# Seven block products for the second expert layer: transposed products, sums per batch, weight blocks kept in DRAM

## The chip, the cores and the metric

The kernel runs on one core of a Trainium2 chip. The metric is device time in microseconds (us), the median of several executions; lower is better. Beside it there is one profiled execution, from which all durations come.

## The reference

Two stages follow one another. The first is attention over 4 batches, 8 heads, 768 positions and head size 64, where a key is kept if it is one of the first `n_global` (8) or among the last `n_local` (96) positions, with a linear distance bias per head. The second is a mixture of four experts on every token: `x` is the attention output as a matrix of 3072 tokens by 512.

```python
p = domain_probs / (domain_probs.sum(-1, keepdims=True) + 1e-09)
for e in range(E):                       # E = 4
    h = np.maximum(x @ w1[e], 0.0)       # 512 -> 1024
    out += p[:, e:e + 1] * (h @ w2[e])   # 1024 -> 512
```

All is in float32. The two products with `w1` and `w2` are most of the arithmetic.

## The kernel before

**Split arithmetic.** A float32 factor is split into a high part (rounded to the matmul format fp32r by a copy on ScalarE) and a low part (the difference, by VectorE or GpSimd). A product is three matmuls: high by high, high by low, low by high. So every weight block and every block of `x` or `h` costs a copy and a subtraction before TensorE may use it.

**Units.** The expert stage goes batch by batch (768 tokens). A unit is one batch, one expert and one group of 256 of the 1024 hidden features; there are 16 units in a batch and 64 in all. `first(i)` makes the 256 hidden features of unit i for 768 tokens, `second(i)` multiplies them with the unit's 256 rows of `w2`.

**First product.** It goes by seven products of blocks (Strassen's scheme in Winograd's form): the 512x256 piece of `w1` is cut in four blocks, `load_w1` builds A11, A12, A22 and the sums S1 to S4 on GpSimd and splits them; `blocks(b)` builds and splits B11, B21, B22 and T1 to T4 of `x`. Each block product is six matmuls with 384 columns (`product`), so a unit has 42. VectorE adds the products up in `add`, four results go through ReLU on ScalarE (`relu`, which also makes the high part of `h`), and VectorE makes the low part (`work_late`).

**Second product.** It is plain: for each of six tiles of 128 tokens, six matmuls with 512 columns have `h` as the stationary side and `w2` as the moving one, so a unit has 36. VectorE multiplies the tile by the expert's share of the token and adds it to `acc`; six such accumulators belong to a batch, and they are written out after its last unit. `load_w2` fetches and splits the unit's `w2` anew for each batch, as `load_w1` does with `w1`.

**Order.** Attention of batch 0 runs first, in program order (`Ordered.on`). From then on the attention of batch b+1 is dealt out in small steps between the products of batch b, and the tile framework's planner, with its own costs, settles the order on each engine. Weight loads, transposed loads and all attention inputs are issued from SP's queue, the outputs from ScalarE's. In every batch the last products of the old batch stand before `blocks(b + 1)`, which has eight VectorE operations in front of the first products of the new one.

**Buffers.** PSUM has eight banks: three for the products (`pm`), two for scores (`ps`), two for transposes (`pt`), one for the attention output (`px`). The weights `w1s` and `w2s` have two buffers each.

Of the kernel before, what the change touches and what calls it, by code (L numbers as in the profile page):

```python
# [18 lines left out]
P = 128  # L19
# [166 lines left out]
def attn_moe_kernel(ctx: ExitStack, tc, q, k, v, n_global, n_local, domain_probs, w1, w2, out):  # L186
# [85 lines left out]
    wp = main.enter_context(tc.tile_pool(name="wp", bufs=2))  # L272
    rp = main.enter_context(tc.tile_pool(name="rp", bufs=1))

    class Pools:


        def __init__(self, stack, name, st, kd, qd, nat, natv, pb, ps, pt):
# [8 lines left out]
            self.pb, self.pT, self.small = sbuf("pb", pb), sbuf("pT", 4), sbuf("small", pb)  # L287
            self.ps, self.pt, self.px = psum("ps", ps), psum("pt", pt), psum("px", 1)

    def mixture():  # L290

        sy.dma_start(prob, domain_probs.rearrange("(t p) e -> p t e", p=P))
        yield
        psumm = fast.tile([P, NT, 1], F32, name="psumm")
        ve.reduce_sum(psumm, prob, axis=AX.X)
        ve.tensor_scalar_add(psumm, psumm, 1e-9)
        ve.reciprocal(psumm, psumm)
        for e in range(E):
            ve.tensor_mul(prob[:, :, e : e + 1], prob[:, :, e : e + 1], psumm)
# [16 lines left out]

    def transpose_half(A, nat, hf):
        tp = A.pt.tile([P, 512], F32, name="pt")
        for t in range(TPH):
            te.transpose(tp[:, t * P : (t + 1) * P], nat[:, hf * TPH + t].rearrange("p j d -> p (j d)"), ident)  # L320
        return tp

    def prepare_q(A, nat, hf, got):

        tp = transpose_half(A, nat, hf)
        st = A.st.tile([P, 2, HALF], F32R, name="st_q")
        ac.activation(st[:, 0, :], tp[:, :HALF], AF.Copy, scale=-SCALE)
        yield
# [8 lines left out]
    def prepare_k(A, nat, hf, got):  # L337


        tp = transpose_half(A, nat, hf)  # L340
# [8 lines left out]
        yield  # L349
# [6 lines left out]
    def prepare_early(A, nat, hf, name, got, zq):  # L356


        tp = transpose_half(A, nat, hf)
# [86 lines left out]
    def weigh(A, three, x):  # L446

        px = A.px.tile([P, 512], F32, name="px")
# [17 lines left out]
    def attention(b, A, early=False):  # L466
# [5 lines left out]
        def flow(new=None):  # L472

            one, two, three, four = tiles
            if new:
                new["ps"] = scores(A, new["t"], gots[new["pr"]], early)
            if three and not early:
                turn(A, three)
# [3 lines left out]
            if four:  # L482
                turned.append(four)
                if len(turned) == TPH:
                    weigh(A, turned, x)
                    turned.clear()
            tiles[:] = [new, one, two, three]

        def start(pr):

            nats[pr] = {n: next(load(A, src, b, pr, n)) for n, src in (("q", q), ("k", k), ("v", v))}

        def prepare(nat, got):

            got["v"] = nat
            q0, q1 = (prepare_q(A, nat["q"], hf, got) for hf in range(2))
            k0, k1 = (prepare_k(A, nat["k"], hf, got) for hf in range(2))
            next(q0)
            yield 1
            next(q0, None)  # L500
            next(k0)
            yield 1
            next(k0, None)
            yield 1
            next(k1)
            yield 1
            nat["vg"] = windows(A, nat["v"])
            next(k1, None)
            next(q1)
            yield 1  # L510
            next(q1, None)
# [72 lines left out]

    xb = {}

    def blocks(b, ks=(0, 1), low=ve):
# [7 lines left out]
        def high(name, src):  # L595
            if lo == 0:
                xb[name] = bp.tile([P, 2, 2, HALF], F32R, name=f"x{name}")
            ac.copy(xb[name][:, 0, lo:hi], src)

        def rest(eng, name, src):  # L600
            eng.tensor_tensor(xb[name][:, 1, lo:hi], src, f32(xb[name][:, 0, lo:hi]), op=ALU.subtract)

        high("B11", b11)
        high("B22", b22)
        ve.tensor_sub(b12, b22, b12)
        rest(po, "B22", b22)
        yield 1
        rest(low, "B11", b11)
        ve.tensor_add(b11, b12, b11)
        high("T2", b11)  # L610
        yield 1
        rest(low, "T2", b11)
        ve.tensor_sub(b22, b22, b11)
        high("T1", b22)
        yield 1
        rest(low, "T1", b22)
        high("T3", b12)
        yield 1
        rest(po, "T3", b12)
        high("B21", b21)  # L620
        ve.tensor_sub(b11, b21, b11)
        yield 1
        rest(po, "B21", b21)
        high("T4", b11)
        yield 1
        rest(low, "T4", b11)
# [3 lines left out]
    NPR = FF // (2 * P)  # L630
    units = [(b, e, g) for b in range(B) for e in range(E) for g in range(NPR)]
    wts = {}

    def load_w1(i, wait=0, lead=5, hold=2):


        if i >= len(units):
            return
        _, e, g = units[i]
        for _ in range(wait):  # L640
            yield 1
        raw = rp.tile([P, KT, 2 * P], F32, name="raw1")
        sy.dma_start(raw, w1[e, :, g * 2 * P : (g + 1) * 2 * P].rearrange("(a p) f -> p a f", p=P))
        for _ in range(lead):
            yield 1
        a11, a21 = raw[:, 0:2, :P], raw[:, 0:2, P:]
        a12, a22 = raw[:, 2:4, :P], raw[:, 2:4, P:]
        sums = rp.tile([P, 4, 2, P], F32, name="sums")
        s1, s2, s3, s4 = (sums[:, n] for n in range(4))
        po.tensor_add(s1, a21, a22)  # L650
        po.tensor_sub(s2, s1, a11)
        po.tensor_sub(s3, a11, a21)
        po.tensor_sub(s4, a12, s2)
        for _ in range(hold):
            yield 1
        dst = wp.tile([P, 2, 7, 2, P], F32R, name="w1s")
        wts[(i, 1)] = {name: dst[:, :, n] for n, name in enumerate(("A11", "A12", "A22", "S1", "S2", "S3", "S4"))}
        for sl, src in (
            (slice(0, 2), raw[:, :, :P].rearrange("p (n a) f -> p n a f", n=2)),
            (slice(2, 3), a22.rearrange("p (n a) f -> p n a f", n=1)),  # L660
            (slice(3, 5), sums[:, 0:2]),
            (slice(5, 7), sums[:, 2:4]),
        ):
            ac.copy(dst[:, 0, sl], src)
            po.tensor_tensor(dst[:, 1, sl], src, f32(dst[:, 0, sl]), op=ALU.subtract)
            yield 1

    def load_w2(i, lead=7):

        if i >= len(units):  # L670
            return
        _, e, g = units[i]
        raw = rp.tile([P, 2, DM], F32, name="raw2")
        sy.dma_start(raw, w2[e, g * 2 * P : (g + 1) * 2 * P, :].rearrange("(a p) m -> p a m", p=P))
        for _ in range(lead):
            yield 1
        dst = wp.tile([P, 2, 2, DM], F32R, name="w2s")
        wts[(i, 2)] = dst
        for f in range(2):
            ac.copy(dst[:, 0, f], raw[:, f])  # L680
            po.tensor_tensor(dst[:, 1, f], raw[:, f], f32(dst[:, 0, f]), op=ALU.subtract)
            yield 1

    hs = {}

    def product(i, a, x):

        pm = ps_mm.tile([P, 512], F32, name="pm")
        m = 0
        for kt in range(2):  # L690
            for wi, xi in ((0, 0), (1, 0), (0, 1)):
                te.matmul(
                    pm[:, :HALF], wts[(i, 1)][a][:, wi, kt, :], xb[x][:, xi, kt, :], start=(m == 0), stop=(m == 5)
                )
                m += 1
        return pm

    late = []

    def work_late():  # L700

        while late:
            lo, src, hi = late.pop()
# [174 lines left out]
```

## Time and profile before

| What | Value |
|---|---|
| median of 3 runs | 1233.19 us (1232.62 to 1234.7) |
| the profiled execution's own time | 1233.96 us |
| its span, first to last instruction | 1232.2 us |
| TensorE (PE) busy | 1182.1 us, 96% |
| VectorE (DVE) busy | 993.0 us, 81% |
| GpSimd (POOL) busy | 737.4 us, 60% |
| ScalarE (ACT) busy | 568.3 us, 46% |
| DMA moved | 117.22 MB, 95 GB/s |

In the rows below, PE is TensorE's matmul, PEld its weight load, DVE VectorE, ACT ScalarE, POOL GpSimd and SP the queue engine. A group's row names the tile written and those read (`pm<-w2s,h`), partitions by elements, the count, the busy time in us, the mean ns of one, and the idle time of the engine before it with what ended it. `xT` and `xB` are the blocks of `x`; `p`, `u`, `vv` and `c` the partial sums of the first product. Almost every row has line 42, that of the helper through which each operation is issued, so groups are told apart by tiles.

### The profile page before, as it was taken

How to read it: one execution, taken by the hardware profiler on the slowest of the kernel's cores; microseconds unless marked ns; L12 is line 12 of the kernel's file. 1: busy time of each engine (PE TensorE's matmuls, PEld its weight loads, DVE VectorE, ACT ScalarE, POOL GpSimd, SP SyncE). 2: the span in 40 equal slices, each digit the busy share in tenths (PEclk: the TensorE clock that was granted, in tenths of full speed). 3: DMA queues.
4: the chain of work that ended last, by engine and by line, in shares of the span. 5: the costliest groups of instructions: out<-in, count | busy, mean ns of one | idle time of the engine just before them, and what ended most of it. 6: DMA issues, size and time to landing. Idle time of an engine off the chain costs nothing.

```text
span 1232.2 us, 18808 instructions
## 1 busy us (share of the span) xinstructions
PE 1182.1 (96%) x6624; PEld 1052.2 (85%) x6624; DVE 993.0 (81%) x2018; ACT 568.3 (46%) x1332; POOL 737.4 (60%) x706
## 2 busy tenths in 40 slices
PE   6779999999999999999998999999999899999997
PEld 4558889889888899899897899889898799999996
DVE  6888898888978888887888887978787876666665
ACT  4764455554543554544543454554454333333321
POOL 5467655655575755655568655655656686666630
PEclk9989999999999999999999999999999999999999
DMA  6324343424324325242412433343331222222211
GB/s 160 103 56 117 94 121 95 121 84 124 94 74 145 103 79 141 78 139 81 126 56 78 149 108 99 105 114 106 100 90 57 103 69 69 69 69 69 69 35 54
DMA packets 142678, 117.22 MB, mean 95 GB/s; under 512 B 82672, under 2 KB 115440, under 8 KB 142576
## 3 DMA queue, kind: packets, MB, share of 16 engines
q1 hardware_dynamic: 138832, 109.65, 31.5%
q10 hardware_dynamic: 3744, 6.30, 1.3%
q8 instruction: 54, 0.88, 0.3%
q14 instruction: 48, 0.39, 0.1%
HBM read 86.03 MB, written 6.29 MB: 75 GB/s over the span
## 4 chain that ended last, share of the span: by engine, by line
PE 85%; DVE 12%; ACT 1%; issue 1%; DMA 0%; ACTq 0%; DVEq 0%
PE pm L42 75%; PE pt L42 4%; PE px L42 3%; DVE pb L42 3%; PE ps L42 3%; DVE h L42 2%; DVE acc L42 1%; DVE u L42 1%; DVE zsum L42 1%; DVE xT L42 1%; ACT pb L42 1%; DVE x L42 1%; DVE vv L42 1%; DVE c L42 0%; DVE early_q L42 0%
## 5 line engine op out<-in xcount | busy, mean ns | idle before, releaser
L42 PE MATMUL pm<-w2s,h 128*128 128x512 f32 x2304 | 557.3, 395 | 15.9 <-DVE acc L42 15.5
L42 PEld LDWEIGHTS pm<-w2s,h 128*128 128x128 f32 x2304 | 427.6, 189 | 109.9 <-DVE acc L42 21.9
L42 POOL TENSOR_TENSOR w1s<-raw,w1s 128x512 fp32r<-128x512 f32 (+1 forms) x128 | 156.1, 1238 | 272.8 <-ACT w1s L42 272.4
L42 DVE SCALAR_TENSOR_TENSOR acc<-pm,prob,acc 128x512 f32<-128x512 f32 x360 | 262.1, 744 | 64.2 <-PE pm L42 62.2
L42 PE MATMUL pm<-xT,w1s 128*128 128x384 f32 x1536 | 297.2, 338 | 3.4 <-DVE xT L42 1.8
L42 PEld LDWEIGHTS pm<-xT,w1s 128*128 128x128 f32 x1536 | 266.6, 188 | 8.1 <-DVE xT L42 2.7
L42 PE MATMUL pm<-xB,w1s 128*128 128x384 f32 x1152 | 228.3, 340 | 0.7 <-DVE xB L42 0.4
L42 PEld LDWEIGHTS pm<-xB,w1s 128*128 128x128 f32 x1152 | 201.7, 188 | 6.9 <-DVE xB L42 0.7
L42 POOL TENSOR_TENSOR w2s<-raw,w2s 128x512 fp32r<-128x512 f32 x128 | 164.9, 1308 | 65.6 <-ACT w2s L42 63.1
L42 POOL TENSOR_TENSOR w1s<-sums,w1s 128x512 fp32r<-128x512 f32 x128 | 167.9, 1331 | 3.3 <-ACT w1s L42 2.9
L42 ACT CAST w2s<-raw 128x512 fp32r<-128x512 f32 x128 | 73.8, 618 | 192.8 <-PE pm L42 183.3
L42 ACT ACTIVATE pb<-pb,nmax 128x256 f32<-128x256 f32 (+1 forms) x192 | 93.1, 486 | 109.1 <-DVE nmax L42 101.8
L42 POOL TENSOR_TENSOR sums<-raw 128x256 f32<-128x256 f32 x128 | 95.0, 763 | 65.1 <-DMA raw<-in_moe_w_dram 65.1
L42 DVE TENSOR_SCALAR pb<-pb,zsum 128x256 f32<-128x256 f32 (+1 forms) x192 | 111.3, 611 | 2.9
L42 ACT ACTIVATE h<-c 128x384 fp32r<-128x384 f32 x64 | 33.6, 525 | 113.0 <-DVE c L42 112.4
L42 DVE TENSOR_TENSOR u<-pm,p 128x384 f32<-128x384 f32 x64 | 35.6, 556 | 58.0 <-PE pm L42 52.4
L42 DVE CUSTOM_DVE_ANT_0 pb<-ps,nbias 128x256 f32<-128x256 f32 (+1 forms) x192 | 71.4, 394 | 7.2 <-PE pt L42 3.7
L42 ACT COPY pT<-pt 128x512 f32<-128x512 f32 (+1 forms) x96 | 52.2, 544 | 52.7 <-PE pt L42 52.4
L42 DVE SCALAR_TENSOR_TENSOR h<-u,h 128x384 fp32r<-128x384 f32 x64 | 66.9, 1046 | 10.0 <-ACT h L42 9.6
L42 ACT CAST w1s<-sums 128x512 fp32r<-128x512 f32 x128 | 74.0, 614 | 1.1 <-POOL sums L42 1.0
L42 DVE TENSOR_TENSOR u<-pm,u 128x384 f32<-128x384 f32 x128 | 70.4, 550 | 3.5 <-PE pm L42 2.9
L42 PE MATMUL pt<-ident,pb 128*128 128x128 f32 x352 | 57.6, 280 | 13.9 <-DVE pb L42 13.2
(87 smaller groups left out, 1276.8 us busy)
## 6 DMA issues: line engine op xcount, KB each, us to landing
raw<-in_moe_w_dram SPq DMA_DIRECT2D x128, 512.0 KB, 3.5
qd<-st_q SPq DMA_DIRECT2D x96, 192.0 KB, 3.5
v<-in_v_dram SPq DMA_DIRECT2D x16, 384.0 KB, 4.1
out_dram<-acc ACTq DMA_DIRECT2D x24, 256.0 KB, 2.3
q<-in_q_dram SPq DMA_DIRECT2D x30, 192.0 KB, 3.1
k<-in_k_dram SPq DMA_DIRECT2D x30, 192.0 KB, 3.6
vg<-v SPq DMA_DIRECT2D x16, 288.0 KB, 3.7
q<-in_q_dram SPq DMA_DIRECT2D x4, 96.0 KB, 3.2
```

The source lines that it names most:

```text
L42: ins = fn(*args, **kwargs)
```

## The change

- **Second product.** Two units make a chunk, 32 in all, eight a batch. `second(c)` multiplies transposed: a block of `w2` is stationary, `h` (features by 384 tokens) is moving. In batches 1 to 3 it goes by seven block products per chunk, of 12 matmuls with 384 columns each (`SCHEME`, `multiply`); in batch 0 it is plain, with 96 such matmuls per chunk.
- **Sums per batch.** Each of the seven products has its own sum in SBUF (`slot`), to which `collect` adds every chunk's product; the scheme's final additions (`FINAL`) are made once per batch. `output` then turns the result with 12 transposes per half batch on TensorE, copies it on ScalarE, and stores 768 KB at a time.
- **Hidden features.** `first` lets products add up in PSUM where it can, and one VectorE operation (`weighed`) does ReLU and the multiplication with the expert's share, which `load_mix` brings from DRAM, spread over all partitions. `hidden(k)` makes the block sums of `h` and splits each 768 wide block: a copy on ACT, and the difference on DVE (all of batch 0; T4 and T1 later) or on POOL (the other five).
- **Weight blocks.** The split blocks of `w1` are made in batch 0 only and those of `w2` in batch 1 only (`make_pair`); each pair of blocks is written to DRAM by a DMA from POOL (`keep`) and read back by SP's queue in the later batches (`pair_w1`, `next_w2`). A pair of `w1` has three buffers to turn in, one of `w2` four (two units by two pairs).
- **Block sums of x.** `blocks(b + 1)` gives one block per step, spread over the last seven steps of the batch before; the first six steps of the new batch's second products are put ahead of its first product (`ALONE`).
- **Attention.** The q and k inputs come in halves with three buffers; scores have one PSUM bank, `px` shares the two of the transposes, and the products have two banks (`ps_mm`) and three more (`y0`, `y1`, `z`).

```diff
-    def blocks(b, ks=(0, 1), low=ve):
+    def blocks(b, A, ks=(0, 1), low=po):
...
+        def split(name, src, eng):
+            high, rest = block(name)
+            ac.copy(high, src)
+            eng.tensor_tensor(rest, src, f32(high), op=ALU.subtract)
...
+    PAIRS1 = (("A11", "A12"), ("S2", "S1"), ("S3", "S4"), ("A22",))
+    PAIRS2 = (("A11", "A12"), ("S3", "A22"), ("S2", "S1"), ("S4",))
+    def split_pair(dst, src):
+        ac.copy(dst[:, 0], src)
+        po.tensor_tensor(dst[:, 1], src, f32(dst[:, 0]), op=ALU.subtract)
...
+        if pair == ("A11", "A12"):
+            po.tensor_add(s1, q[:, 0, 1], q[:, 1, 1])
+            po.tensor_sub(s2, s1, q[:, 0, 0])
+            split_pair(dst, q[:, :, 0])
...
+    def keep(key, dst, shape):
+        kept[key] = dp.tile(shape, F32R, name="kept_" + "_".join(str(n) for n in key))
+        po.dma_start(f32(kept[key]), f32(dst))
...
+        dst = wts1[j] = w1p.tile(shape, F32R, name="w1p")
+        if b > 0:
+            sy.dma_start(f32(dst), f32(kept[(1, e, g, n)]))
...
+            dst = wts2[(c, n, u)] = w2p.tile(shape, F32R, name="w2p")
+            if b == 0:
+                split_pair(dst, raws2[(c, n, u)])
+            elif b == 1:
+                q = raws2[(c, u)].rearrange("p n (m f) -> p n m f", m=2)
+                make_pair(dst, PAIRS2[n], q, sums2[(c, u)])
+                keep((2, e, g, n), dst, shape)
+            else:
+                sy.dma_start(f32(dst), f32(kept[(2, e, g, n)]))
...
+        def weighed(n, src):
+            mix = mixes[(b, e, int(n[1]) - 1)].rearrange("p t q -> p (t q)")
+            ve.scalar_tensor_tensor(h[n], src, 0.0, mix, op0=ALU.max, op1=ALU.mult)
...
+        def add(n, pm, other):
+            ve.tensor_add(h[n], pm[:, :HALF], other)
+            weighed(n, h[n])
...
+    SCHEME = (("A11", "11"), ("A12", "21"), ("S3", "T3"), ("A22", "T4"), ("S2", "T2"), ("S1", "T1"), ("S4", "22"))
...
+    def hidden(k):
+            eng = ve if name in ("T4", "T1") else po
+            if name == "T3":
+                ve.tensor_sub(h["12"], h["22"], h["12"])
+            elif name == "T4":
+                ve.tensor_add(h["11"], h["12"], h["11"])
+                ve.tensor_sub(h["21"], h["21"], h["11"])
+            elif name == "T1":
+                ve.tensor_sub(h["12"], h["22"], h["11"])
...
+        dst = splits[k] = (tp2 if third else sp2).tile([P, 2, 2, HALF], F32R, name="third" if third else "hs")
+        ac.copy(dst[:, 0], src)
+        eng.tensor_tensor(dst[:, 1], src, f32(dst[:, 0]), op=ALU.subtract)
...
+    def collect(pm, b, n, m, new):
+        dst = slot(b, n)[:, m]
+        if new:
+            ac.copy(dst, pm[:, :HALF])
+        else:
+            ve.tensor_add(dst, pm[:, :HALF], dst)
...
+        for n, (a, _) in enumerate(SCHEME):
+            hidden(k0 + n)
+            if n < 6 or not last:
+                hidden(k0 + n + 1)
+            for m in range(2):
+                pm = ps_mm.tile([P, 512], F32, name="pm")
+                multiply(pm, c, PLACE2[a], splits[k0 + n], m, True, True)
+                collect(pm, b, n, m, nc_ == 0)
+                yield
+            if n in (1, 3, 5, 6):
+                next_w2()
```

In the loop over batches, one first-product step (six matmuls) and, from three steps after a chunk's hidden features on (`LAG`), about one second-product step (also six matmuls) alternate; attention steps are dealt out as before.

More of the change, by code (lines that the diff above doesn't have):

```diff
@@ L651, in load_w1 @@
[L651 to L666, printed above, removed]
@@ new lines, in pair_w1, with load_w2 @@
+        q = raws1[i].rearrange("p (n a) (m f) -> p n m a f", n=2, m=2)
+        make_pair(dst.rearrange("p s n (a f) -> p s n a f", a=2), PAIRS1[n], q, sums)
+        keep((1, e, g, n), dst, shape)
+    seq2 = [(c, n) for c in range(NCH) for n in (range(2) if c < CPB else range(4))]
+    made2 = [0]
+    def load_w2(c, n):
+        b = c // CPB
+        if c >= NCH or b > 1 or (b == 1 and n > 0):
+            return
+        for u in range(2):
+            _, e, g = units[2 * c + u]
+            w = w2[e, g * F4 : (g + 1) * F4, :].rearrange("(n p) m -> p n m", p=P)
+            if b == 0:
+                raws2[(c, n, u)] = rp.tile([P, 2, F4], F32, name="half")
+                sy.dma_start(raws2[(c, n, u)], w[:, :, n * F4 : (n + 1) * F4])
+            else:
+                raws2[(c, u)] = rp.tile([P, 2, DM], F32, name="raw")
+                sums2[(c, u)] = rp.tile([P, 2, F4], F32, name="sums")
+                sy.dma_start(raws2[(c, u)], w)
@@ L743, in attn_moe_kernel @@
-    accs = {}
-    def second(i):
-        b, e, g = units[i]
-        w2s, h = wts[(i, 2)], hs[i]
-        for t in range(NQT):
-            pm = ps_mm.tile([P, 512], F32, name="pm")
-            n = 0
-            for f in range(2):
-                for hi, wi in ((0, 0), (0, 1), (1, 0)):
-                    te.matmul(
-                        pm, h[:, hi, f, t * P : (t + 1) * P], w2s[:, wi, f, :], start=(n == 0), stop=(n == 5)
-                    )
-                    n += 1
-            work_late()
-            w = prob[:, b * NQT + t, e : e + 1]
-            if e == 0 and g == 0:
-                acc = op.tile([P, DM], F32, name=f"acc{t}")
-                accs[(b, t)] = acc
-                ve.tensor_scalar_mul(acc, pm, w)
-            else:
-                acc = accs[(b, t)]
-                ve.scalar_tensor_tensor(acc, pm, w, acc, op0=ALU.mult, op1=ALU.add)
-            if e == E - 1 and g == NPR - 1:
-                r0 = b * S + t * P
-                ac.dma_start(out[r0 : r0 + P, :], acc)
-            yield
@@ L802, in attn_moe_kernel @@
-    per = E * NPR
-    count, span = NPAIR * (6 + NQT) + 5, (13 * per - 12) * 0.97
-    Ordered.on = True
-    chores.append(blocks(0, (1,)))
-    for _ in range(2):
-        work_chores()
+    up = main.enter_context(tc.tile_pool(name="up", bufs=2))
+    ap = main.enter_context(tc.tile_pool(name="ap", bufs=1))
+    sp2 = main.enter_context(tc.tile_pool(name="hs", bufs=2))
+    tp2 = main.enter_context(tc.tile_pool(name="third", bufs=1))
+    ps_h = main.enter_context(tc.tile_pool(name="ps_h", bufs=1, space=PSUM))
@@ new lines, in attn_moe_kernel, with step_second @@
+    ps_mm = main.enter_context(tc.tile_pool(name="ps_mm", bufs=2, space=PSUM))
+    A = Pools(main, "att", st=1, kd=1, qd=1, nat=3, natv=1, pb=2, pT=3, ps=1, pt=2, px=0)
+    LAG, ALONE = 3, 6
+    per = 7 * PER
+    count, span = NPAIR * (6 + NQT) + 5, per - 9
+    firsts = (s for i in range(len(units)) for s in first(i))
+    seconds = [second(c) for c in range(NCH)]
+    xblocks = blocks(0, A, (1,))
+    Ordered.on = True
+    next(xblocks)
+    next(xblocks)
+    chunk, credit = 0, 0.0
+    def step_second():
+        nonlocal chunk
+        while chunk < NCH and state["done"] >= min(14 * (chunk + 1) + LAG, 7 * len(units)):
+            if next(seconds[chunk], 0) is None:
+                return True
+            chunk += 1
+        return False
@@ L836, in attn_moe_kernel @@
+                next(xblocks)
+            credit += 8 / 7 if chunk < CPB else 1
+            while credit >= 1:
+                credit = credit - 1 if step_second() else 0
+            while emitted < count and emitted * (span - begin) < (done - begin) * count:
+                next(att, None)
+                emitted += 1
+    while step_second():
+        pass
     main.close()
```

448 lines of the change are left out of this document (284 added, 164 removed).

## The prediction

> **What bounds the kernel now.** I read the page's first and fourth parts, then the busy time by stretches (the five are the start and the four batches), then the timeline of PE.
>
> ```profile
> span 1232.2 us, 18808 instructions
> PE 1182.1 (96%) x6624; PEld 1052.2 (85%) x6624; DVE 993.0 (81%) x2018; ACT 568.3 (46%) x1332; POOL 737.4 (60%) x706
> PE 85%; DVE 12%; ACT 1%; issue 1%; DMA 0%; ACTq 0%; DVEq 0%
> ```
>
> PE sets the end: 85% of the chain that ended last is its own work. The next rows give, for each stretch, the busy time of PE, PEld, DVE, ACT and POOL (instructions in brackets), the granted clock, the DMA share and GB/s.
>
> ```profile
> 0.00:95.00 95.00, 68.19 (x459) 53.65 (x460) 75.03 (x250) 59.05 (x171) 54.08 (x70) 0.95 0.43 104
> 95.00:379.00 284.00, 277.66 (x1577) 247.15 (x1576) 243.88 (x490) 139.44 (x326) 174.98 (x165) 0.99 0.37 102
> 379.00:675.00 296.00, 290.58 (x1661) 260.73 (x1660) 249.02 (x502) 143.34 (x336) 180.82 (x168) 1.00 0.36 104
> 675.00:971.00 296.00, 291.18 (x1657) 260.75 (x1656) 247.98 (x501) 143.10 (x335) 180.79 (x167) 0.99 0.35 99
> 971.00:1233.00 262.00, 254.45 (x1277) 229.93 (x1275) 177.10 (x279) 83.33 (x166) 146.69 (x140) 0.99 0.21 69
> ```
>
> A full batch takes 296 us; PE is busy for 290.6 of them, DVE for 249.0 (84%), POOL for 180.8 (61%). What a matmul costs in steady work must be read from starts, since records of matmuls overlap. The timeline of PE in the last batch (start, length, instructions):
>
> ```profile
> 1069.37 8.36 PE L42 MATMUL pm<-w2s,h 128*128 128x512 f32 x36
> 1077.57 1.23 PE L42 MATMUL pm<-xB,w1s 128*128 128x384 f32 x6
> 1078.63 3.28 PE L42 MATMUL pm<-xT,w1s 128*128 128x384 f32 x18
> 1081.75 2.24 PE L42 MATMUL pm<-xB,w1s 128*128 128x384 f32 x12
> ...
> 1084.87 8.36 PE L42 MATMUL pm<-w2s,h 128*128 128x512 f32 x36
> ```
>
> A unit repeats every 1084.87 - 1069.37 = 15.50 us: 36 matmuls of 512 columns in 1077.57 - 1069.37 = 8.20 us (0.2278 each) and 42 of 384 in the other 7.30 us (0.1738 each). There is no gap in it, so here time is the number of matmuls by their width.
>
> **The change on PE.** Two units take 2 x 15.50 = 31.0 us now. The first products stay at 84 matmuls. The second ones go from 72 of 512 columns to 84 of 384 in batches 1 to 3: 14.60 us in place of 16.40, so -1.80, and for 24 chunks -43.2 us. In batch 0 they go to 96 of 384: 16.68, +0.28, for 8 chunks +2.2 us. The outputs cost 96 transposes that were not there. Their price:
>
> ```profile
> 571.42 0.49 PE L42 MATMUL pt<-ident,q 128*128 128x128 f32 x3
> 571.75 0.60 PE L42 MATMUL pt<-ident,pb 128*128 128x128 f32 x4
> ```
>
> Three take 0.33 us, so 96 cost +10.6 us. PE's sum is **-30.4 us**. Attention keeps its matmuls.
>
> **Do the other engines keep up?** Groups with shapes (busy us, mean ns | idle before):
>
> ```profile
> L42 DVE SCALAR_TENSOR_TENSOR acc<-pm,prob,acc 128x512 f32<-128x512 f32 x360 | 262.1, 744 | 64.2 <-PE pm L42 62.2
> L42 DVE TENSOR_TENSOR u<-pm,u 128x384 f32<-128x384 f32 x128 | 70.4, 550 | 3.5 <-PE pm L42 2.9
> L42 DVE SCALAR_TENSOR_TENSOR h<-u,h 128x384 fp32r<-128x384 f32 x64 | 66.9, 1046 | 10.0 <-ACT h L42 9.6
> L42 DVE SCALAR_TENSOR_TENSOR h<-p,h 128x384 fp32r<-128x384 f32 x64 | 40.4, 630 | 1.3 <-ACT h L42 0.7
> L42 DVE TENSOR_TENSOR x<-x 128x768 f32<-128x768 f32 x12 | 14.4, 1200 | 2.7 <-ACT x L42 2.7
> L42 DVE TENSOR_TENSOR xT<-x,xT 128x768 fp32r<-128x768 f32 x9 | 16.5, 1834 | 0.0
> L42 POOL TENSOR_TENSOR w2s<-raw,w2s 128x512 fp32r<-128x512 f32 x128 | 164.9, 1308 | 65.6 <-ACT w2s L42 63.1
> L42 POOL TENSOR_TENSOR w1s<-raw,w1s 128x256 fp32r<-128x256 f32 x64 | 63.8, 997 | 3.0 <-ACT w1s L42 3.0
> L42 POOL TENSOR_TENSOR sums<-raw 128x256 f32<-128x256 f32 x128 | 95.0, 763 | 65.1 <-DMA raw<-in_moe_w_dram 65.1
> L42 POOL TENSOR_TENSOR xB<-x,xB 128x768 fp32r<-128x768 f32 x6 | 12.0, 2025 | 1.2 <-ACT xB L42 1.2
> L42 ACT CAST xB<-x 128x768 fp32r<-128x768 f32 x9 | 7.4, 826 | 0.0
> ```
>
> DVE, for two units before: 14 adds from PSUM at 0.55, eight low parts of `h` at 0.6 to 1.05 (two at 1.05, six near 0.63), twelve accumulations at 0.744: 7.7 + 5.9 + 8.9 = 22.5 us; a batch 180, so attention and the blocks of x are 249 - 180 = 69. After, in a chunk by seven products: in the first products eight operations from PSUM at 0.55 and six `weighed` on `h` at 0.63; four block sums of `h` at 1.20; two differences at 1.83; 14 additions in `collect` at 0.55: 4.4 + 3.8 + 4.8 + 3.7 + 7.7 = 24.4 us, a batch 195 + 69 = 264. PE's new batch is 296 less 14.4, plus 24 transposes (2.6), less what the boundary below gives, near 280. DVE comes to 94% in place of 84%. It is still below PE, but its slack shrinks by two thirds.
>
> The two rows of `h` show the same shape at 0.63 and 1.05 us, while `u<-pm,u`, which reads PSUM, keeps 0.55. The Trainium skill (SBUF — State Buffer, Who interferes with whom) says that a VectorE instruction with two SBUF inputs and a GpSimd instruction that reads SBUF exclude each other for the whole instruction. The trace agrees (1046 against 630 ns). By that rule a 2.03 us split on POOL, the new kind, holds DVE up longer than today's 1.31 us one, and the 24.4 us would grow in batch 1 and shrink in batches 2 and 3, where POOL has less to do; by the rows alone it is 24.4 everywhere.
>
> POOL, by batch: five 768 wide splits per chunk cost 8 x 5 x 2.03 = 81 us in batches 1 to 3. The blocks of one weight cost per unit four sums at 0.76 and splits worth 3 x 1.31 + 1.0, 8.0 us, in 16 units 128 us (w2 in batch 1; w1 in batch 0 has one pair split by halves, 3 x 1.0 in place of 1.31 + 1.0, so 139, and w2 is split there plain, 32 x 1.31 = 42). Its DMA issues do not stand in this trace. The nearest rows are SP's and the landings:
>
> ```profile
> L42 SPq DMA_DIRECT2D qd<-st_q x32: 467/590/1220, 391.7 to 609.1; - x32
> raw<-in_moe_w_dram SPq DMA_DIRECT2D x128, 512.0 KB, 3.5
> out_dram<-acc ACTq DMA_DIRECT2D x24, 256.0 KB, 2.3
> ```
>
> I take 0.59 us per issue on POOL, between 0 (the queue hides it) and 1.22; 64 in a batch are 38 us. Batch 0 is then some 228 with windows and blocks, batch 1 81 + 128 + 38 + the same 9 = 256 of 280, batches 2 and 3 about 90. The Trainium skill (DMA: Bandwidth & Descriptors, Specifications and SWDGE vs HWDGE vs iDMA) says that such a DMA has its descriptors computed in software on GpSimd, with about 1 us to the first byte against 0.6; by that, as an estimate, 64 us, and batch 1 stands at 282 of 280, the case of the slower rival below. No run here shows it yet.
>
> So batch 1 is the tight one, and bursts count there, not only sums. After product T1 of a chunk POOL must make the next chunk's first pair of `w2` (two splits 2.6, four sums 3.0, two issues 1.2) and the next split of `h` (2.03): 8.8 us. PE covers this with five groups of six matmuls, 5.2 us, and attention's share: 290.6 busy less 16 x 15.5 leaves 42.6 in a batch of 224 groups, 0.19 each, so 6.1 in all. If nothing is done ahead PE is 2.7 us late, and at the next product (two sums 1.5, two splits 2.6, issues 1.2, split 2.0: 7.3 against four groups' 4.9) again 2.4. The sums need only the raw rows, so they can be pulled forward; with them gone both waits nearly close. I take **+9** for batch 1, from 0 to +41 (8 x 5.1).
>
> **What else moves.** *The batch boundary.* At it PE now waits for DVE, which has eight block operations queued:
>
> ```profile
> 662.52 2.13 DVE L42 TENSOR_TENSOR xT<-x,xT 128x768 fp32r<-128x768 f32 x1
> ...
> 667.90 0.50 PE L42 MATMUL pm<-w2s,h 128*128 128x512 f32 x1 [3.59 <-DVE acc L42]
> ```
>
> With the blocks spread over seven steps, and six second-product steps in reserve, these waits go: three boundaries, up to -11; I take **-10** (0 if the fuller DVE is late there all the same). *Reading weights back.* In batches 2 and 3 both weights come from DRAM, 1.8 MB each per unit (seven 128x2x2x128 blocks of 4 bytes), 58 MB in 280 us, 207 GB/s. The last stretch moved 69 GB/s at a share of 0.21, so 329 at full; 207 is 0.63. The old weights are 1 MB a unit, 57 GB/s in 296 us, 0.17, so attention has 0.36 - 0.17 = 0.19: 0.82 in all, and in batch 1, with 29 MB of writes, about 0.9. The first pair of `w2` is asked for when T1's matmuls end: two 512 KB reads, 3.5 us for one by the row and 1.6 for the second, 5.1 against the same cover of 6.1. I take **+2**, from 0 to +24 (16 chunks late by 1.5). What waits on SP behind such a read are attention's inputs and the transposed q. The first q of this batch is issued at 391.7 us (row above), and PE uses it at 402.5, so 10.8 us later:
>
> ```profile
> L42 PE MATMUL ps<-kd,qd x96: 274/281/284, 402.5 to 627.6; 128*128 128x256 f32 x96
> ```
>
> That covers a read of 5 us, and the step is costed at nothing; without that cover a late q would stop PE 8 times a batch.
>
> *The end.* The last chunk has no first products beside it: ScalarE's copy (0.83) and POOL's split (2.03) stand against two groups of six (2.1), 0.8 to 1.0 late for each of five; then a DVE add, a final sum, transposes, and 768 KB to land in place of 256. I take **+8** (+3 to +14). *The start.* The first 17 steps are first products alone; POOL needs per unit 9 us and the issues against 7.3 of PE: **+3**, from -6 to +10, since PE idles there today as well.
>
> Edits costed at nothing: one bank for scores and none for `px` (a batch has 53 attention steps, one per 5.6 us), additions inside PSUM, ReLU on DVE (counted above), and ScalarE's seven copies per chunk (7 x 0.83, on an engine that is busy for 143 of 296 us). If that cover goes, they show as PE waiting for ACT or DVE at `pt` or `y`.
>
> **Sum.** -30.4 + 9 - 10 + 2 + 8 + 3 = -18.4. The profiled execution took 1233.96 us, so 1215.6; the median of the runs is 0.8 lower, so **1215 us**.
>
> **Rivals.** *Nothing new waits* (20%): PE's sum and the boundary arrive, the rest is hidden, the end costs +3: 1233.2 - 30.4 - 10 + 3 = 1196. For it: the last batch runs without a gap; against it: DVE at 94%. *Slower, POOL in batch 1* (19%): the burst above is not spread, 5.1 us in each of 8 chunks, 41 in place of 9: 1247. It decides from 27/8 = 3.4 us per chunk on. For it: POOL at 256 of 280 us with unknown issues; against it: the planner can pull the sums forward, and PE has first products to go on with. *The weights come late* (7%): reads 1.5 us late in 16 chunks, +22: 1237, as before within the uncertainty or slower. Against it: a DMA share of 0.82.
>
> **How the numbers follow.** The forecast has 54%, with its own range 1198 to 1230. A difference of 0.2%, 2.5 us, is what can be told from no change. Faster by that: all of the second case and nearly all of the first, 71%; same 7%, from the third and the edges; slower 22%. The range 1188 to 1248 leaves a tenth out at each end: DVE's or POOL's burst beyond the whole 41 above, a smoother PE below.
>
> **What would show it.** Groups of six matmuls with 384 columns should follow each other at 0.174 us; 84 second-product matmuls a chunk in batches 1 to 3; a batch of near 280 us for 2 and 3. If the stretch of batch 1 is longer than that of batch 2, POOL is the place; PE waiting for a DMA in batches 2 and 3 would show the third rival; DVE over 95% where POOL is free would mean that I undercounted DVE. A median over 1231 makes the forecast wrong, and so does PE work that does not fall by 30 us.

## The result: 1360.6 us against 1234.0

The changed kernel takes 1360.59 us in the median of 4 runs (1357.23 to 1372.88); the kernel before, run beside it, 1233.95. The ratio is 1.104, with a 95% interval from 1.0966 to 1.1114. I had forecast 1215, faster. The profiled execution is the one of 1372.88 us, 12 above the median, so what follows describes a run with somewhat more waiting than the usual one.

The page of the kernel after: span, busy time, granted clock, and the chain that ended last.

```profile
span 1371.1 us, 20747 instructions
PE 1210.3 (88%) x7201; PEld 1148.8 (84%) x7201; DVE 988.5 (72%) x1919; ACT 588.5 (43%) x1271; POOL 664.6 (48%) x624
PEclk9989999999999988989998999999999999999999
PE 54%; DVE 18%; DMA 11%; POOL 9%; issue 5%; ACT 4%; SPq 0%; ACTq 0%; DVEq 0%; POOLq 0%
```

PE's share of the chain fell from 85% to 54%, and no other engine took over: DVE is busy for 72%, POOL for 48%. This is a kernel that waits, in turns, for everything. The busy time by stretches (start, four batches cut at the first product of each, and the tail; columns as in the prediction) says where:

```profile
80.00:392.00 312.00, 285.49 (x1750) 273.43 (x1750) 228.15 (x424) 158.18 (x359) 210.89 (x242) 0.97 0.62 192
392.00:755.00 363.00, 303.95 (x1742) 290.05 (x1741) 262.20 (x462) 153.66 (x331) 212.00 (x202) 0.90 0.65 208
755.00:1081.00 326.00, 294.29 (x1781) 280.24 (x1780) 250.02 (x496) 138.87 (x296) 112.55 (x79) 0.96 0.73 231
1081.00:1324.00 243.00, 237.93 (x1364) 234.31 (x1365) 162.48 (x265) 77.88 (x123) 79.40 (x42) 1.00 0.73 250
1324.00:1371.00 47.00, 31.80 (x161) 26.86 (x160) 26.65 (x38) 11.76 (x16) 17.56 (x9) 0.94 0.35 125
```

Cut at the same points, the batches took 306, 295 and 296 us before; now 312, 363 and 326. Batch 1, in which the blocks of `w2` are made and written, loses 68 us; batch 2, which starts with the last second products of batch 1, 30.

PE busy hides the loss, because a matmul at half clock counts as longer work. So I split PE's time from the starts of all its matmuls: each is charged its steady interval (0.173 us for 384 columns, 0.2265 for 512, 0.1195 for 256, 0.109 for 128, 0.051 for the attention output; the scores of batch 0's attention at their own median there, 0.216); what exceeds this inside stretches of granted clock 0.5 is half clock, the rest is waiting. The totals are good to some 3 us, differences between kernels to about 1.

| us, whole span | work | half clock | waits | waits by stretch: start, batches 0 to 3, tail |
|---|---|---|---|---|
| before | 1137.5 | 6.3 | 76.6 | 28.8, 20.8, 13.0, 12.8, 1.2, 0 |
| after | 1108.6 | 44.3 | 207.3 | 28.2, 38.4, 73.3, 46.6, 8.4, 12.6 |

The work fell by 28.9 us. Waits rose by 130.7 and half clock by 38.0: in all +139.8, and the spans differ by 138.9.

The waits of the kernel after (us in total, times, longest):

```profile
POOL hs L42 <- ACT hs L42: 372.8, 88, 22.2
...
DVE h L42 <- POOL hs L42: 109.2, 57, 8.0
...
PE pm L42 <- DVE sums_lo L42: 30.1, 16, 5.5
PE ps L42 <- DMA qd<-st_q: 25.2, 9, 4.5
```

The first row is idle time of POOL itself. Two things are new. VectorE waits 57 times for a low part of `h` on POOL, because the next block sum (44 times), or the next chunk's `h` (13 times), is written over the block that POOL still reads. And PE waits for VectorE's addition from PSUM (`sums_lo`) and for the transposed q, for which it never waited before.

One such wait, on three engines (timelines of VectorE, POOL and PE after: start, length, instruction):

```profile
503.08 6.80 DVE L42 TENSOR_SCALAR pb<-pb,zsum 128x256 f32<-128x256 f32 x2
509.81 0.54 DVE L42 TENSOR_TENSOR h<-y,part 128x384 f32<-128x384 f32 x1
```

```profile
503.45 0.57 POOL L42 DMA_DIRECT2D kept<-w2p  x1
504.04 1.30 POOL L42 TENSOR_TENSOR w2p<-raw,w2p 128x512 fp32r<-128x512 f32 x1
505.30 1.81 POOL L42 TENSOR_TENSOR hs<-h,hs 128x768 fp32r<-128x768 f32 x1
507.05 0.57 POOL L42 DMA_DIRECT2D kept<-w2p  x1
507.65 1.81 POOL L42 TENSOR_TENSOR hs<-h,hs 128x768 fp32r<-128x768 f32 x1
```

```profile
504.83 1.20 PE L42 MATMUL z<-xT,w1p 128*128 128x384 f32 x6
511.56 2.26 PE L42 MATMUL pm<-hs,w2p 128*128 128x384 f32 x6 [5.52 <-DVE sums_lo L42]
```

Two small VectorE operations in SBUF, which the page's group has at 0.57 us on average, last 6.80 us together and end 0.4 us after POOL's fifth instruction in a row. All that VectorE owes PE stands behind them, and PE stops for 5.5 us. When it comes back, six matmuls take 2.26 us instead of 1.2: half clock. In the whole trace 20 VectorE operations last over 2.5 us (up to 6.5). The 13 over 3 us lie between 99 and 806 us, the time in which writes are issued, and each stands beside an issue or begins within 0.3 us of its end. Before there was none over 2.14 us.

### The profile page after: what moved, and what is told of

The parts are those of the page before. It is cut to its first block, busy times and chain, and to the rows that moved or that the text cites. A ratio compares the mean times of both kernels' runs of the same rounds, so it can differ in the third digit from the quotient of the medians.

```text
span 1371.1 us, 20747 instructions
## 1 busy us (share of the span) xinstructions
PE 1210.3 (88%) x7201; PEld 1148.8 (84%) x7201; DVE 988.5 (72%) x1919; ACT 588.5 (43%) x1271; POOL 664.6 (48%) x624
## 4 chain that ended last, share of the span: by engine, by line
PE 54%; DVE 18%; DMA 11%; POOL 9%; issue 5%; ACT 4%; SPq 0%; ACTq 0%; DVEq 0%; POOLq 0%
PE pm L42 24%; PE y L42 16%; PE z L42 7%; DVE h L42 7%; PE pt L42 4%; DMA qd<-st_q 4%; POOL hs L42 3%; PE ps L42 3%; DVE pb L42 2%; POOL w2p L42 2%; DMA raw<-in_moe_w_dram 2%; DVE sums_lo L42 2%; DVE zsum L42 1%; DMA w2p<-kept 1%; ACT pb L42 1%
## 5 line engine op out<-in xcount | busy, mean ns | idle before, releaser
L42 PE MATMUL pm<-hs,w2p 128*128 128x384 f32 x2544 | 536.4, 346 | 63.1 <-DVE sums_lo L42 27.4
L42 PEld LDWEIGHTS pm<-hs,w2p 128*128 128x128 f32 x2544 | 459.4, 194 | 81.1 <-issue 17.7
L42 POOL TENSOR_TENSOR hs<-h,hs 128x768 fp32r<-128x768 f32 x120 | 225.6, 1881 | 409.0 <-ACT hs L42 372.8
L42 PE MATMUL y<-xT,w1p 128*128 128x384 f32 x1152 | 252.3, 353 | 23.9 <-DVE h L42 12.9
L42 ACT CAST hs<-h 128x768 fp32r<-128x768 f32 x190 | 158.6, 835 | 214.3 <-PE pm L42 185.7
L42 PEld LDWEIGHTS y<-xT,w1p 128*128 128x128 f32 x1152 | 209.4, 197 | 29.8 <-DVE h L42 14.5
L42 PE MATMUL y<-xB,w1p 128*128 128x384 f32 x768 | 164.8, 347 | 5.3 <-POOL w1p L42 2.5
L42 DVE SCALAR_TENSOR_TENSOR h<-h,mix 128x384 f32<-128x384 f32 x192 | 164.6, 857 | 3.9
L42 DVE TENSOR_TENSOR sums_lo<-pm,sums_lo 128x384 f32<-128x384 f32 x224 | 122.2, 550 | 52.4 <-PE pm L42 51.6
L42 PEld LDWEIGHTS y<-xB,w1p 128*128 128x128 f32 x768 | 135.4, 193 | 9.4 <-POOL w1p L42 3.1
L42 PE MATMUL ps<-kd,qd 128*128 128x256 f32 x288 | 54.8, 307 | 28.8 <-DMA qd<-st_q 25.2
```

Of the source, the lines that this page charges most:

```text
L42: ins = fn(*args, **kwargs)
```

## The experiments

The theory with which I began: a write issued from POOL's queue does more than hold POOL for 0.57 us, it shuts VectorE out for several of POOL's instructions. Its rivals: the traffic to DRAM is to blame, whichever queue issues it; the low parts of `h` on POOL stand in a chain with VectorE; making the blocks of `w2` on POOL with one product of lead comes late (the slower rival of the prediction); late q; attention beside a fuller schedule. The split of PE's time for the main runs, as above:

| us | median | ratio to before (95%) | work | half clock | waits |
|---|---|---|---|---|---|
| after | 1360.59 | 1.104 (1.0966 to 1.1114) | 1108.6 | 44.3 | 207.3 |
| writes from SP | 1328.31 | 1.0752 (1.0732 to 1.0771) | 1108.6 | 27.9 | 178.4 |
| and low parts of `h` on VectorE | 1296.40 | 1.05 (1.0455 to 1.0546) | 1108.6 | 26.0 | 149.0 |
| writes from SP, second product plain | 1306.53 | 1.0567 (1.0541 to 1.0594) | 1158.4 | 17.6 | 118.3 |
| before, with writes from POOL | 1300.48 | 1.051 (1.0463 to 1.0558) | 1137.5 | 25.3 | 130.7 |
| before, with writes from SP | 1245.10 | 1.0078 (1.0061 to 1.0095) | 1137.5 | 6.8 | 88.6 |
| before, `w1` blocks kept | 1225.75 | 0.9921 (0.9904 to 0.9939) | 1137.5 | 5.2 | 66.4 |

**1. The writes from ScalarE's queue.**

```diff
-        po.dma_start(f32(kept[key]), f32(dst))
+        ac.dma_start(f32(kept[key]), f32(dst))
```

> Theory A (the writes issued from GpSimd: while their descriptors are made, GpSimd keeps the SBUF port it shares with VectorE over several of its own instructions, VectorE stands for 3 to 6.5 us, PE runs dry and loses its clock): with the same 128 writes issued from ScalarE's queue, no VectorE operation above 2.7 us in batches 0 and 1, batch 1 falls from 363 us to 310 or less, the whole to about 1290 us. Theory B (the splits of h on GpSimd and the two buffers they turn in: VectorE waits for GpSimd to have read h before it may overwrite it): nothing of that is touched, 1345 to 1365 us. Theory C (DMA load: late q, late weights): the same bytes move, 1350 to 1365 us.

1349.34 us, ratio 1.0927 (1.0909 to 1.0946). The long VectorE operations are gone (longest 2.6 us), as theory A has it, yet little time came back: the time is that of theory B, not the 1290 of A. What ScalarE now holds up in their place I did not isolate.

**2. The writes from SP's queue.** The same line with `sy.dma_start`.

> The same with the writes issued from SP's queue. Theory A: like the run with ScalarE's queue, about 1290 us; if SP's queue, which also fetches weights and attention inputs, is held up by waiting for each split, some of it comes back as PE waiting for DMA (1290 to 1320). Theories B and C: 1345 us or more.

1328.31 us, 32 below the median of after (36 by the ratios, and the interval of after alone is 9 us to each side), with the same transfers and bytes. The longest VectorE operation takes 2.6 us. The time lies between the forecasts, above the 1320 of A and below the 1345 of its rivals. VectorE still waits for POOL's low parts as often:

```profile
DVE h L42 <- POOL hs L42: 125.7, 61, 6.7
```

**3. The kernel before with such writes added, from POOL.** The blocks of `w1` of units 0 to 31 are written to DRAM as they are split, and never read.

```diff
             po.tensor_tensor(dst[:, 1, sl], src, f32(dst[:, 0, sl]), op=ALU.subtract)
+            if i < 32:
+                spare = dp.tile([P, 2, sl.stop - sl.start, 2, P], F32R, name=f"spare_{i}_{sl.start}")
+                po.dma_start(f32(spare), f32(dst[:, :, sl]))
```

> The kernel before with nothing added but 128 writes from GpSimd's queue: in batches 0 and 1 each split block of w1 is also written to DRAM and never read. Theory A: VectorE operations of 3 us and more appear in these batches alone, and the kernel gets slower by 20 to 60 us. Theories B and C: below 10 us slower (GpSimd has room for 64 issues of 0.57 us a batch, and the DMA queues are at a third).

1300.48 us: 128 writes cost the tuned kernel 66 us, 0.5 us each, with no other change. Again 20 VectorE operations last over 2.5 us (up to 5.7), all while writes are issued. The issues hold POOL longer here, 0.80 us in the median, but PE never waits for POOL: what it waits for is VectorE (first before, then this run).

```profile
PE pm L42 <- DVE acc L42: 15.5, 10, 3.6
PE pm L42 <- DVE acc L42: 55.6, 35, 4.0
```

One of these places, in the timelines of VectorE, POOL and PE:

```profile
612.38 3.77 DVE L42 TENSOR_SCALAR pb<-pb,zsum 128x256 f32<-128x256 f32 x2
616.07 1.40 DVE L42 SCALAR_TENSOR_TENSOR acc<-pm,prob,acc 128x512 f32<-128x512 f32 x2
```

```profile
611.77 1.39 POOL L42 DMA_DIRECT2D spare<-w1s  x2
612.95 2.77 POOL L42 TENSOR_TENSOR w1s<-sums,w1s 128x512 fp32r<-128x512 f32 x2
615.43 1.65 POOL L42 DMA_DIRECT2D spare<-w1s  x2
```

```profile
616.87 1.42 PE L42 MATMUL pm<-w2s,h 128*128 128x512 f32 x5 [1.52 <-DVE acc L42]
```

**4. The control: the same writes from SP.** `po.dma_start` becomes `sy.dma_start`.

> The control: the kernel before with the same 128 writes issued from SP's queue. Theory A: within 5 us of the kernel before, no VectorE operation above 2.2 us. If the bytes or the buffers are what costs, it is as slow as the run that issues them from GpSimd.

1245.1 us, +10 (I had expected at most 5), and no VectorE operation over 2.2 us; VectorE is busy for 996 us, in run 3 for 1062. So of the 66 us some 55 belong to the queue that issues, 10 to the traffic and to SP. In the kernel before the direct cost of a POOL-issued write is therefore shown; in the changed kernel the same move is worth 32 us. That other waits stand behind the one that goes is likely, and not shown.

**5. All low parts of `h` on VectorE,** on top of 2.

```diff
-            eng = ve if name in ("T4", "T1") else po
+            eng = ve
```

> On the kernel with writes from SP's queue (1328 us): all differences of the split blocks of h on VectorE, none on GpSimd. Theory B (VectorE stands waiting for GpSimd's 1.85 us splits of h, 126 us in all, and hands the delay on to PE): VectorE no longer waits for GpSimd at h, PE waits fall, 1290 us or less, although VectorE gets 5 x 0.95 us more per chunk. Theory D (VectorE is simply short of time beside attention): more work on it makes it worse, 1335 us or more.

1296.4 us, another 32 less (the forecast of B was 1290 or less). VectorE's busy time rises from 941 to 996 us and PE waits less, so VectorE's load was not the cost. The edit takes away two things at once. One is POOL as a station between two VectorE operations: VectorE no longer waits for POOL at `h`. The other is POOL's work beside VectorE: 120 more low parts take 115 us of VectorE, yet its busy time rises by 54, since its other operations in SBUF got shorter, for instance this one (number 2, then this run):

```profile
L42 DVE TENSOR_SCALAR pb<-pb,zsum 128x256 f32<-128x256 f32 x160 | 82.7, 551 | 2.5
L42 DVE TENSOR_SCALAR pb<-pb,zsum 128x256 f32<-128x256 f32 x160 | 65.6, 443 | 2.1
```

How the 32 us divide between the two, no run here shows. What PE still waits for:

```profile
PE ps L42 <- DMA qd<-st_q: 14.1, 7, 3.5
PE pm L42 <- POOL w2p L42: 11.6, 7, 3.0
PE y L42 <- ACT part L42: 9.6, 4, 4.2
PE pm L42 <- DVE sums_lo L42: 9.2, 11, 3.1
```

No one cause is left. Against before this kernel has 28.9 us less work, 19.7 more at half clock and 72.4 more waits: 10 in batch 0, 24 in batch 1, 22 in batch 2, 7 in batch 3 and 10 in the tail, with 2 less at the start.

**6. The second product plain in all batches,** on top of 2: transposed as in batch 0, 96 matmuls a chunk, `w2` fetched and split in every batch, nothing of it kept. The core of the edit:

```diff
-        if b == 0:
+        if True:
             k0 = 4 * c
-    plain = 4 * CPB
+    plain = 4 * NCH
```

> On the same kernel: the second product plain in all four batches (still transposed), so seven-product sums, splits on GpSimd, the larger sums per batch, and the DRAM copies of w2 are gone. PE has 24 x 2.08 = 50 us more matmuls. Theory B (the block sums and splits of h and their order are the cost): waits fall to those of batch 0, and the time is about 1108.6 + 50 + 100 = 1260 to 1290 us, faster than 1328 in spite of the work. Theory E (the transposed layout, the shared banks and the DRAM copies of w1 cost it): waits stay, 1340 to 1380 us.

1306.53 us, between the two forecasts. Its low parts of `h` are all but two on VectorE, so number 5 is the one to compare with: the seven products, with the making and keeping of their blocks of `w2`, save 49.8 us of matmuls and give 39 of them back, 30.7 in waits and 8.4 at half clock. The scheme is worth 10 us here, where its matmuls promise 50. And the transposed layout with the kept blocks of `w1`, without seven products of `w2`, is already 72 us above before, 21 of it matmuls.

**7. The transposed q from ScalarE's queue,** on top of 2.

```diff
-                sy.dma_start(f32(qd[n * D : (n + 1) * D, j]), f32(st[j * D : (j + 1) * D]))
+                ac.dma_start(f32(qd[n * D : (n + 1) * D, j]), f32(st[j * D : (j + 1) * D]))
```

> On the same kernel: the transposed q is issued from ScalarE's queue, so that it does not stand behind weight reads on SP's. Theory C (late q beside a DMA load of 0.7): PE no longer waits for q, some 15 to 25 us faster, 1305 to 1315. If q is late only in the wake of VectorE's delays: within 6 us of 1328.

1370.19 us, ratio 1.1081 (1.1056 to 1.1106), 42 more, which neither theory had. PE's waits for q grew from 9.3 us in number 2 to 41.1. Another queue does not bring q earlier; ScalarE's own order brings it later.

**8. A third buffer for split `h` and a lead of two,** on top of 2. The room is taken from one transposed-probability buffer, one half-row buffer and one mixing buffer.

> On the same kernel: three buffers for the split blocks of h and each block asked for two products ahead (room for it from one buffer less for pT, the half rows of w2 and the expert shares). Theory B in the form that the lead of one product is too short: ScalarE's wait for PE's release and with it PE's wait for the splits go, 1280 to 1300 us. Theory D: unchanged, 1320 to 1335.

1362.7 us, ratio 1.1024 (1.0998 to 1.105), 34 more, which neither theory had. Batch 0, where the second product is plain, waits 52.4 us in place of some 30, so the room that was taken costs by itself, and the run says nothing certain on the lead. Taking the room alone was not tried.

**9. Two buffers for q, and its second half one step earlier,** on top of 5, the room taken in the same way.

> On the kernel with writes from SP's queue and all splits of h on VectorE (1296 us): two buffers for the transposed q and its second half made one attention step earlier (room from one buffer less for pT, the half rows of w2 and the expert shares). Theory C (late q costs PE 14 us of waiting and the clock after it): no wait for q, 1270 to 1285 us. If the smaller buffers or the order take their place: 1290 us or more.

1315.78 us, ratio 1.0664 (1.062 to 1.0708), 19 more. The waits for q are gone, but batch 0 waits 49.8 us in place of some 31. The same confounding; the wait for q is removed by a buffer, at a price paid elsewhere.

**10. After, without the attention of batches 1 to 3.**

```diff
-        att = attention(b + 1, A) if b + 1 < B else iter(())
+        att = iter(())
+        xs[b + 1] = xs[0]
```

> The changed kernel without the attention of batches 1 to 3, whose experts work on what is left of the x of batch 0; all else, the writes from GpSimd too, stays. PE loses 3 x 43 us of work. Theory F (the change loses only where attention's VectorE and ScalarE steps meet its handovers): batches 2 and 3 take about 240 us each with waits below 10 us, batch 1 keeps the cost of GpSimd's writes (250 to 280); the whole 1060 to 1100 us. Theory B alone (handovers are late whatever runs beside them): batch 2 keeps some 30 us of waits, the whole 1130 us or more.

1224.59 us, far above what it would be if the losses came with attention: 180.5 us of waits are left of 207.3. From about 753 us on, two groups of six matmuls take 2.08 us and nothing stops them for long stretches (timeline of PE):

```profile
820.50 1.20 PE L42 MATMUL pm<-hs,w2p 128*128 128x384 f32 x6
821.54 1.20 PE L42 MATMUL z<-xB,w1p 128*128 128x384 f32 x6
822.58 1.20 PE L42 MATMUL pm<-hs,w2p 128*128 128x384 f32 x6
```

The losses sit where blocks are still made: batch 0, batch 1 and the first 85 us of batch 2. Batch 2 waits 30 us, as theory B has it.

**11. Number 6 with the blocks of `w1` made anew in every batch,** no copies in DRAM.

> On the kernel with the plain second product in all batches (1306 us): the blocks of w1 are made anew in every batch, nothing is written to DRAM or read back. Theory C (DMA load makes q and the weights late): the waits for q go and it gets 10 to 25 us faster. If VectorE's and GpSimd's shared port costs as much as the DMA load did: within 8 us of 1306.

1319.35 us, ratio 1.0683 (1.0662 to 1.0704), 13 more, outside both forecasts. PE waits 18.7 us for q here and 19.7 in number 6, so in this kernel the traffic of the kept blocks is not what makes q late.

**12. The kernel before with only the blocks of `w1` kept:** split in batch 0, written from SP, read back in batches 1 to 3 as one transfer of 1.8 MB.

```diff
+        if i >= E * NPR:
+            ...
+            dst = wp.tile([P, 2, 7, 2, P], F32R, name="w1s")
+            sy.dma_start(f32(dst), f32(kept[(e, g)]))
...
+        kept[(e, g)] = dp.tile([P, 2, 7, 2, P], F32R, name=f"kept_{e}_{g}")
+        sy.dma_start(f32(kept[(e, g)]), f32(dst))
```

> The kernel before with one part of the change alone: the split blocks of w1 are made in batch 0, written from SP's queue, and read back as one 1.8 MB transfer in batches 1 to 3. Theory C: the reads make q late here too, 1240 to 1260 us. If DMA load harms only beside the rest of the change: GpSimd and ScalarE are relieved of 128 us and 53 us a batch, and with them VectorE's port, so 1220 to 1234 us.

1225.75 us, ratio 0.9921 (0.9904 to 0.9939): below both kernels. Its batches 1 and 2:

```profile
384.00:676.00 292.00, 289.65 (x1664) 261.33 (x1663) 220.47 (x502) 114.85 (x272) 51.13 (x39) 1.00 0.56 179
676.00:968.00 292.00, 289.81 (x1667) 261.70 (x1666) 220.28 (x501) 116.32 (x274) 50.46 (x39) 1.00 0.53 173
```

From first product to first product a batch takes some 291 us, 5 less than before, with the same matmuls: POOL is busy for 51 us in place of 181, VectorE, less hindered, for 220 in place of 249, and PE's waits fall from 13.0 and 12.8 us to 8.6 and 8.4. The row of `h` that took 1046 ns before shows it:

```profile
L42 DVE SCALAR_TENSOR_TENSOR h<-u,h 128x384 fp32r<-128x384 f32 x64 | 41.4, 647 | 5.5 <-ACT h L42 2.3
```

**13. Number 5 without the attention of batches 1 to 3,** the edit of number 10.

> The kernel with writes from SP's queue and all splits of h on VectorE (1296 us), without the attention of batches 1 to 3, whose experts work on what is left of the x of batch 0. Theory F (once GpSimd is out of the way, the rest of the loss is attention meeting the handovers): batches 1 and 2 wait less than 15 us each, and the whole is 1075 to 1100 us. Theory B in its general form (one product of lead is too short even alone): some 30 us of waits stay in batches 1 and 2, 1130 us or more.

1145.52 us, ratio 0.926 (0.9227 to 0.9294). More than theory F has, and more than the 30 us of B: in batches 1 and 2 PE waits 47 us, against 72 with attention. The two largest causes:

```profile
PE pm L42 <- POOL w2p L42: 14.9, 12, 3.4
PE y L42 <- DMA w1p<-kept: 9.8, 7, 3.4
```

So of the waits left in these batches after the two repairs a third goes with attention, and two thirds are there without it, led by the making of the blocks and their late reads.

**14. Number 12 with the blocks of `w2` kept too.**

> The kernel before with the split blocks of w1 and of w2 made in batch 0, written from SP's queue and read back in batches 1 to 3 (w1 alone: 1226 us). If the relief of GpSimd's port is what gained: another 1 to 5 us, 1219 to 1226. If the added 1 MB a unit makes q or the weights late: 1228 us or more.

1254.27 us, ratio 1.0148 (1.0124 to 1.0172). Batches 1 and 2 wait 9.1 and 9.0 us, no less than in number 12, and batch 0 waits 45 in place of 18 while it writes 2.9 MB per unit. So the reads did no harm, and the loss is in the batch of the writes. Keeping is not good in itself; that it paid in number 12 because POOL's work had been in VectorE's way fits the rows, and was not tried by itself.

## Why the prediction was wrong

| Step of the prediction | predicted, us | measured |
|---|---|---|
| PE's work | -30.4 | -28.9 |
| batch 1, POOL's burst | +9 (0 to +41) | waits +60.3 in after, +24.4 in number 5 |
| boundary | -10 (0 to -11) | none; a wait of 6.4 at 401, 4.4 at 748, 3.5 at 1069 |
| reading back, batches 2 and 3 | +2 (0 to +24) | waits +41.0 in after, +28.9 in number 5, in part the end of batch 1's blocks |
| start, with batch 0 | +3 (-6 to +10) | waits +17.0 in after, +8.6 in number 5 |
| end | +8 (+3 to +14) | waits +12.6 in the tail |
| half clock | no term | +38.0 |

(Each stretch holds the boundary waits that fall in it.) PE's sum was right: 384 columns at 0.173 us, a chunk by 84 matmuls, the transposes. It was the covers that failed.

**The step that failed first** is "I take 0.59 us per issue on POOL". The size was right, the row has 0.57:

```profile
L42 POOL DMA_DIRECT2D kept<-w2p x64 | 35.8, 560 | 8.0 <-POOL w2p L42 5.0 <-issue 2.4 <-PE y L42 0.3
```

and POOL's sum of batch 1 was not exceeded: POOL is busy for 212.0 us in that stretch, 53 of the 64 issues among them, where I had 256. The other estimate, 64 us for the 64 issues, does not come out: the row has 35.8. But I priced a write as time of POOL alone, and as late weights at worst. Runs 3 and 4 show the price on VectorE: 66 us for 128 writes, 10 for the same ones from SP. No row of the trace of before could show it, since nothing was issued from POOL there; my bounds of 0 to 1.22 us on POOL were bounds for the wrong engine. The Trainium skill (SBUF — State Buffer, SBUF: two separate sides) says that whichever of a conflicting VectorE and GpSimd operation starts first keeps the shared ports for its whole instruction and that the other blocks. The trace of before agrees: no VectorE operation lasts beyond 2.14 us, and an operation of that shape takes 0.94 us at the least, so there is room in it for about one POOL instruction. In the runs with POOL-issued writes it does not hold so: VectorE waits through two to five instructions in a row. Why the issue keeps VectorE from its turn in between, no run here shows.

**The second** is the sum for VectorE and POOL, "24.4 us" for two units and "81 us" of low parts on POOL, where I asked whether they keep up and not in which order they go. Their loads were not exceeded: VectorE is busy for 250 us in the stretch of batch 2, where I had 264. But a block of `h` is added in place, its copy is split on POOL, and the next sum waits for that split: 109 us of VectorE's time, 57 times, and what PE needs from PSUM stands behind it. The prediction had named the rule that the two engines hinder each other, and gave it no term. Moving the splits to the engine that I thought was the fuller one gained 32 us, with that hindrance in it.

**The slower rival** had the right place, batch 1, and the point from which it decides, 3.4 us per chunk; it was given 19% and at most 41 us. With writes and low parts out of the way, its own mechanism is still there: PE waits for POOL's `w2p` 11.6 us in number 5 and 14.9 in number 13. That pulling the sums forward would have both waits "nearly close" had no row behind it. The third rival, weights that come late, has little of its own: in the kernel after PE waits 9.3 us, in eight waits, for blocks read back.

**The late q** was costed at nothing by the first q of a batch and its 10.8 us of cover. The later ones have less. SP's and PE's timelines after:

```profile
522.39 4.44 SPq L42 DMA_DIRECT2D qd<-st_q  x4
```

```profile
530.76 0.77 PE L42 MATMUL ps<-kd,qd 128*128 128x256 f32 x2 [3.60 <-DMA qd<-st_q]
```

The four are issued from 522.4 to 526.8; PE could use the first at 527.2 and goes on at 530.8, 8.4 us after the first issue. Landing takes 5.1 us in the median, 3.5 before. I took the cover of the kernel before for that of the new one: from the first issue of such a group to the time when PE could use it, the trace of before has 7.5 us or more in all 24 groups, the trace after less than 5.3 in 11 of them. The shorter lead, more than the traffic, makes q late: in run 11 q lands in 3.6 us in the median, about as before, but 12 groups have 4.3 us or less; in run 12 it lands in 4.5, with 5.0 or more for every group, and PE waits 2.1 us for q in all. What shortens the lead in the new order stays open.

**The half clock** was left out altogether. The granted clock around one wait for q (times in us, columns as above), and PE's row:

```profile
446.80:450.90 4.10, 0.89 (x6) 0.57 (x4) 0.35 (x1) 0.00 (x0) 0.00 (x0) 1.00 0.96 312
451.00:457.80 6.80, 5.57 (x22) 4.97 (x24) 0.71 (x4) 2.78 (x6) 0.00 (x0) 0.50 0.51 167
458.00:465.00 7.00, 6.64 (x49) 5.47 (x45) 2.56 (x10) 3.07 (x10) 0.00 (x1) 1.00 0.64 211
```

```profile
452.23 0.77 PE L42 MATMUL ps<-kd,qd 128*128 128x256 f32 x2 [4.54 <-DMA qd<-st_q]
```

A wait of 4.5 us, from 447.7 to 452.2, brings 6.8 us at half clock from 450.9 on. PE works through the last 5.5 of them and loses 2.8 us more, so this wait costs 1.6 times its length; over the kernel the factor is 38.0/130.7, 0.29 on top. The trace after has 24 such periods, of 3.4 or 6.8 us but for the last one, the trace before 5. The Trainium skill (TensorE: Matmul & The Clock Gate, Part 1: The HAM clock gate) has half rate after an idle window of about 3.4 us and full rate after a busy one. The trace agrees on the one half and on multiples of 3.4 us, but not on an idle window of that length: seven of the 24 periods follow a single wait of 2.2 to 2.5 us, with no longer one in the 7 us before. Other waits of 2.3 to 2.5 us, at 139 and 203 us for instance, bring none.

**The boundary** gained nothing: "these waits go" took VectorE's eight operations as the only thing there. With those spread, ScalarE's copy and VectorE's additions from PSUM come late in their place, 6.4 and 4.4 us. Before the copy ScalarE itself waits 4.7 and 1.5 us for rows of `w2` (`half`) that it has to split first. **The end** was right in kind and near the upper bound.

What stays open: how the 72 us of waits that number 5 has above before divide between block making, reads, q and attention, beyond the thirds of run 13 for batches 1 and 2, and whether a longer lead would help, since both attempts at it (8 and 9) took room that cost more.

## What to carry to other kernels

When a scheme saves matmuls by more block sums, splits and copies, price the order in which they hand blocks to each other, operation by operation with the buffer that each overwrites, and not only each engine's sum: here no engine's sum was exceeded, and PE still lost 131 us to new waits. Add a term for the half clock to every new wait of some microseconds. Keep transfers off GpSimd's queue while VectorE works in SBUF beside it, and when a part of a change is cheap to try alone, as keeping the blocks of `w1` was, try it alone: among the complete kernels here it was the only one that got below before.

## What the runs showed of the hardware

- A DMA issued from POOL takes 0.57 us of POOL in the kernel after and 0.80 in run 3, but 20 VectorE operations beside 128 of them lasted 2.5 to 6.5 us (2.6 to 5.7 in run 3), through several POOL instructions. The same transfers issued from SP do not do this: 1300.5 against 1245.1 us in otherwise equal kernels.
- The queue that issues matters: the same writes give 1360.6 from POOL, 1349.3 from ScalarE and 1328.3 from SP.
- Reading back 29 MB of split blocks per batch beside attention (DMA share 0.56, 179 GB/s) does not slow a kernel whose matmuls leave no gap; with POOL's making of these blocks gone in its place the kernel gained 9.5 us.
- The clock was halved after waits well under 3.4 us: seven of the 24 periods of granted clock 0.5 in the kernel after follow a single wait of 2.2 to 2.5 us.
